# Ways in and out of a long convolution as fixed rounds, with the ranking of its mixture of experts moved into the middles

## Chip, cores and metric

The kernel runs on one core of a Trainium2 chip. The metric is the device time of one execution in microseconds, the median of three runs.

## What is computed

A gated long convolution in fp32 feeds a two-level mixture of experts. Shapes: 4 batches, 10048 positions, 128 channels; the experts' stage sees 40192 tokens, 4 groups of 4 experts, hidden size 1024.

```python
h_filt = (relu(pos_emb @ w1) @ w2) * exp(-0.01 * pos)[:, None]
u = x * v
y = irfft(rfft(u, 2 * S) * rfft(h_filt, 2 * S))[:, :S]
t = (x * y).reshape(B * S, D)
g = argmax(t @ w_group); e = argmax(t @ w_expert[g])
out = g_weight * e_weight * (relu(t @ w1[g, e]) @ w2[g, e])
```

## The kernel before

The transform is done by matmuls, and one batch of 128 channels fits into two tiles in SBUF, `z` and `zr` (frequencies from 64 on). Each batch passes through three kinds of work, all in `conv`:

- the way in: 43 parts of 3 channels. `product` loads x and v (tile `xv`, SP's queue, line 462) and multiplies them on VectorE (line 467); ScalarE writes a negated half (line 478) and VectorE folds both into `eo` (line 480), which is `fold`. `dft_blocks` multiplies `eo` with a table on TensorE (line 412, 6 matmuls a part, two instructions each), and ScalarE copies the result into `z` and `zr` (line 425).
- the middle, or way through: 40 steps over pairs of frequencies. `middle` transforms over positions (line 497), multiplies with the filter's spectrum on VectorE (lines 660 and 663, tile `t`), and POOL adds (lines 661 and 664, tile `y`); `back` transforms back (line 673), and ScalarE copies into `z` (line 680).
- the way out: 22 groups of 6 channels (the last two of 4), two groups sharing one set of transposes. `turned` transposes `z` on TensorE (lines 692 and 695) and copies to tiles `tt` on ScalarE (line 697), `inverse_rest` starts the sums for two `po` buffers (line 707), `inverse_blocks` loads `xo`, the other factor, from `x_out` (line 723, ScalarE's queue; line 725, SP's, for the last batch), finishes the sums (line 728), has ScalarE copy halves crosswise into `oo` (lines 737 and 738), adds on VectorE (`yt`, line 743) and multiplies with `xo` into `xy` (line 745).

The way in of batch b and the way out of batch b - 1 are one loop over the 22 groups. In this text, way 1 is batch 1 in and batch 0 out, middle 1 the way through of batch 1, and so on to way 3 and middle 3; the last way only goes out.

Beside this runs the routing of the batch before. `chosen` sends `xy` to DRAM, computes the router's logits and picks experts; `ranked` (line 857) gives every token its row in a table of pages: about 80 to 110 VectorE instructions, most of them on 128x16 tiles, some two dozen on 128x316 ones. Both are generators; `next(routing, None)` in `conv` takes a step. A step of `chosen` is taken 22 times, so in a middle of 40 places, 27 of which take a step, 5 steps of `ranked` come in the middle, the rest in the next way, one in each group.

When `ranked` has the addresses, it appends to `self.scatters`: 8 clears (line 393) and 79 puts (line 378), indirect DMAs that POOL issues, 128 rows of 520 bytes each. `scatter` sends some at each step, each after ScalarE's latest copy (`pace`); `stage` loads the rows (`stg`, line 367).

The order on each engine comes from a scheduler (the tile layer) that may move an instruction ahead of another. `keep_in_program_order` (called through `in_turn`, too) holds the instructions so marked in the order written. Before, VectorE's product and fold, ScalarE's copies of line 425 and the first matmul of a way are marked; transposes, inverse matmuls, `oo`, `yt` and `xy` are not.

Of the kernel before, what the change touches and what calls it, by code (L numbers as in the profile page):

```python
# [149 lines left out]
class Kernel:  # L150
# [60 lines left out]
    def conv(self, ctx, right):  # L211
# [27 lines left out]
        for b in range(self.nbat + 1):  # L239
            last = b == self.nbat  # L240
            if last:
                ahead.close()
                inner.close()
                self.sp = ctx.enter_context(tc.tile_pool(name="stream", bufs=2, reuse_waits="tile"))
                weights = self.first_weights(right)
            if b > 0:
                xy = xyp.tile([128, NB, D], F32, tag="xy", name=f"xy{b - 1}")
            parts = groups(D, GD) if not last else []
            if b == 1:
                self.router_consts()  # L250
            self.run_ahead(b, 0, made, folded)
            for j, (d0, n) in enumerate(OUTS):
                if b > 0 and j % 2 == 0:
                    tts = self.turned(d0, min(2 * GI, D - d0))
                for i in range(2 * j, min(2 * j + 2, len(parts))):
                    self.run_ahead(b, i, made, folded)
                    self.scatter(1 + (i >= 12 and i % 2))
                    self.dft_blocks(*folded[i])
                    if b > 0 and i % 2 == 0:
                        if j % 2 == 0:  # L260
                            pos = self.inverse_rest(min(2 * GI, D - d0), tts)
                        self.inverse_blocks(b - 1, xy, d0, n, tts, pos[j % 2], j % 2)
                if last:
                    if j % 2 == 0:
                        pos = self.inverse_rest(min(2 * GI, D - d0), tts)
                    self.inverse_blocks(b - 1, xy, d0, n, tts, pos[j % 2], j % 2)
                    next(weights, None)
                    if j == 8:
                        self.scatter(sum(1 for s in self.scatters if s[0] < self.nbat - 2))
                        for p in self.all[:XG]:  # L270
                            p.load()
                for _ in range(3 if last else 1):
                    next(routing, None)
                if last:
                    self.scatter(1 + j % 2)
            made, folded = [], []
# [127 lines left out]
    def dft_blocks(self, b, eo, d0, n, other=False):  # L404
# [4 lines left out]
        for i in range(n):  # L409

            for h, hs in enumerate(HALVES):
# [3 lines left out]
                if d0 == i == h == 0 and b not in ("h", 0):  # L415
                    self.tc.keep_in_program_order(ins)
# [14 lines left out]
    def run_ahead(self, b, i, made, folded):  # L431
# [4 lines left out]
        while len(folded) < min(len(parts), i + AHEAD + 1):  # L436
            folded.append(self.fold(*made[len(folded)]))
# [6 lines left out]
    def product(self, b, d0, n):  # L444
# [15 lines left out]
        else:  # L460
# [3 lines left out]
            if b > 0:  # L464
                self.minus[d0] = xv[:, :n].rearrange("p d a q -> p d (a q)")
        first = b == 0 and d0 < FIRST
        self.in_turn(b, (nc.gpsimd if first else nc.vector).tensor_tensor(xt, xt, vt, ALU.mult))
        return xt, b, d0, n

    def fold(self, xt, b, d0, n):  # L470
# [5 lines left out]
        if b:  # L476
            both = self.minus.pop(d0)
            self.in_turn(b, nc.scalar.activation(both[:, :, 128:192], hi, AF.Copy, scale=-1.0))
# [203 lines left out]
    def turned(self, d0, n):  # L682
# [4 lines left out]
        for s, m in [(None, n // 4)] + groups(n, 4):  # L687
            pt = self.psT.tile([128, 4, 128], F32, tag="pt", name="pt")
            for i in range(m):
                if s is None:  # L690
                    src = self.zr[:, d0 + 4 * i : d0 + 4 * i + 4].rearrange("p d k s -> p (d k s)")
                    nc.tensor.transpose(pt[:, i], src, self.ident)
                else:
                    src = self.z[:, d0 + s + i].rearrange("p k s -> p (k s)")
                    nc.tensor.transpose(pt[:, i], src, self.ident)
# [3 lines left out]
        return tts  # L699

    def inverse_rest(self, n, tts):

        pos = [self.psO.tile([128, GI, NB], F32, tag="po", name="po") for _ in range(2)]
        for g in range(n // 4):
            for h, hs in enumerate(HALVES):
                for po, rs in zip(pos, HALVES):
                    self.nc.tensor.matmul(
# [5 lines left out]
                    )  # L713
        return pos

    def inverse_blocks(self, b, xy, d0, n, tts, po, run):

        nc, d, sp = self.nc, self.d, self.sp
        rows = lambda t: t[:, : n * NB].rearrange("p (t d) -> p t d", d=n)
        xo = sp.tile([128, GI * NB], F32, tag="spec", name="xo", bufs=NSPEC - (b == self.nbat - 1))  # L720
        src = d["x_out"][b, :, d0 * NB : (d0 + n) * NB]
        if b < self.nbat - 1:
            nc.scalar.dma_start(xo[:, : n * NB], src)
        else:
            self.tc.keep_in_program_order(nc.sync.dma_start(xo[:, : n * NB], src))
        for c in range(n):
            for h, hs in enumerate(HALVES):
                nc.tensor.matmul(
                    po[hs, c],
                    tts[1 + c // 2][:, 2 * run + c % 2, hs],  # L730
                    self.fi[:, h, 0],
                    start=False,
                    stop=c == n - 1,
                )
        oo = rows(sp.tile([128, GI * NB], F32, tag="oo", name="oo"))
        by_row = po[:, :n].rearrange("p d t -> p t d")
        nc.scalar.activation(oo[0:64], by_row[64:128], AF.Copy, scale=-1.0)
        ins = nc.scalar.copy(oo[64:128], by_row[0:64])
        if b == self.nbat - 1:
            self.pace = ins  # L740
        pool, tag, bufs = (self.ap, "y", NY) if b < self.nbat - 1 else (sp, "yt", 2)
        yt = rows(pool.tile([128, GI * NB], F32, tag=tag, name="yt", bufs=bufs))
        nc.vector.tensor_tensor(yt, by_row, oo, ALU.add)
        helped = b == self.nbat - 1 and d0 // GI % 2 > 0
        ins = (nc.gpsimd if helped else nc.vector).tensor_tensor(
            xy[:, :, d0 : d0 + n], yt, rows(xo), ALU.mult
        )
        if helped:
            self.beyond(ins)


# [105 lines left out]
    def ranked(self, b, oh, en):  # L857
# [4 lines left out]
        v = nc.vector  # L862
# [320 lines left out]

class Unit:
# [274 lines left out]
```

## Time and profile before

| what | value |
|---|---|
| median of three runs | 2073.45 us (2071.23 to 2076.63) |
| the profiled execution, its own time | 2074.26 us |
| its span | 2072.5 us |
| TensorE matmuls / weight loads busy | 1933.1 us (93%) / 1756.5 us (85%) |
| VectorE / ScalarE / POOL busy | 1592.8 / 1424.9 / 1304.2 us |
| DMA | 391.34 MB, 189 GB/s on average |
| first expert matmul starts (line 1307) | 1003.8 us |

The span runs from the profile's first to its last instruction; the execution's own time is 1.8 us longer. The filter and batch 0's way in and middle fill the first 249 us, the ways and middles of this text the stretch from there to 976 us, and the experts' stage is the rest, from about 1004 us on. Busy shares over the whole span are averages over stages with different limits, so a stage has to be read by itself. A busy TensorE is not one at its peak, since matmuls overlap and their ends are modelled.

### The profile page before, as it was taken

The numbers are of one execution on the slowest core, as the hardware profiler recorded it, in microseconds if no ns is written. First come the engines' busy times: TensorE is split into PE (matmuls) and PEld (weight loads), VectorE is DVE, ScalarE is ACT, GpSimd is POOL, SyncE is SP. The second block draws the span as 40 slices with busy tenths as digits, with TensorE's granted clock in tenths as the row PEclk, the third lists the DMA queues.
The fourth block names the chain that finished last, engine by engine and source line by source line (L and its number), as shares of the span: only waits on it lengthen the run. The fifth ranks groups of instructions, "written<-read, shape, count | busy, mean of one in ns | idle before, by whom it ended". The sixth has DMA issues, their size and how long they took to land. (4 is left out here: it accounts for less than half of the span.)

```text
span 2072.5 us, 53304 instructions
## 1 busy us (share of the span) xinstructions
PE 1933.1 (93%) x17518; PEld 1756.5 (85%) x17518; DVE 1592.8 (77%) x3478; ACT 1424.9 (69%) x3395; POOL 1304.2 (63%) x1355
## 2 busy tenths in 40 slices
PE   8988999988898889987999999999999999999997
PEld 7877888777676767766798999999999999999997
DVE  5587676796569855882799997777999998888885
ACT  6652487456543654345787888878888888888885
POOL 3257602655698457956276777878888886555554
PEclk9999999999999999988899999999999999999998
DMA  4699877977897778856654455555555544444442
GB/s 136 224 268 268 260 193 243 309 210 213 228 331 225 219 207 289 288 172 199 219 184 136 142 147 149 155 180 154 162 156 160 156 144 128 134 123 127 127 121 65
DMA packets 260158, 391.34 MB, mean 189 GB/s; under 512 B 32839, under 2 KB 132914, under 8 KB 259872
## 3 DMA queue, kind: packets, MB, share of 16 engines
q1 hardware_dynamic: 226464, 320.47, 51.9%
q0 software_dynamic: 23904, 51.83, 7.2%
q10 hardware_dynamic: 9504, 15.54, 2.8%
q8 instruction: 142, 2.33, 0.5%
q14 instruction: 144, 1.18, 0.2%
HBM read 305.70 MB, written 83.04 MB: 188 GB/s over the span
## 5 line engine op out<-in xcount | busy, mean ns | idle before, releaser
L1316 DVE SCALAR_TENSOR_TENSOR hl<-ph,hh 128x512 fp32r<-128x512 f32 x656 | 446.0, 685 | 126.5 <-ACT hh L1315 98.3
L1315 ACT ACTIVATE hh<-ph 128x512 fp32r<-128x512 f32 x656 | 395.0, 606 | 137.4 <-PE ph L1309 54.2
L378 POOL DMA_INDIRECT prow<-stg,adr x316 | 342.7, 1084 | 153.8 <-issue 60.3
L1352 POOL DMA_INDIRECT out<-os,to x328 | 355.2, 1083 | 92.5 <-issue 81.3
L1326 PE MATMUL py<-hh,wh 128*128 128x256 f32 x1312 | 398.0, 303 | 0.0
L1307 PE MATMUL ph<-xh,wh 128*128 128x256 f32 x1312 | 373.2, 284 | 7.9 <-DVE hl L1316 4.5
L1328 PE MATMUL py<-hh,wl 128*128 128x256 f32 x1312 | 372.4, 284 | 7.3 <-POOL wl L1296 7.3
L1309 PE MATMUL ph<-xh,wl 128*128 128x256 f32 x1312 | 373.4, 285 | 0.3 <-DVE wl L1296 0.3
L1308 PE MATMUL ph<-xl,wh 128*128 128x256 f32 x1312 | 372.6, 284 | 0.0
L1327 PE MATMUL py<-hl,wh 128*128 128x256 f32 x1312 | 370.8, 283 | 0.0
L1296 POOL TENSOR_TENSOR wl<-ws,wh 128x512 fp32r<-128x512 f32 x162 | 218.9, 1351 | 214.5 <-ACT wh L1289 166.5
L1307 PEld LDWEIGHTS ph<-xh,wh 128*128 128x128 f32 x1312 | 252.4, 192 | 8.9 <-ACT hh L1315 4.6
L1328 PEld LDWEIGHTS py<-hh,wl 128*128 128x128 f32 x1312 | 250.7, 191 | 10.0 <-POOL wl L1296 9.9
L1309 PEld LDWEIGHTS ph<-xh,wl 128*128 128x128 f32 x1312 | 252.7, 193 | 1.2 <-DVE wl L1296 1.2
L1308 PEld LDWEIGHTS ph<-xl,wh 128*128 128x128 f32 x1312 | 252.7, 193 | 0.1
L1327 PEld LDWEIGHTS py<-hl,wh 128*128 128x128 f32 x1312 | 252.1, 192 | 0.0
L1326 PEld LDWEIGHTS py<-hh,wh 128*128 128x128 f32 x1312 | 251.3, 192 | 0.0
L1296 DVE TENSOR_TENSOR wl<-mw,wh 128x512 fp32r<-128x512 f32 x318 | 231.1, 727 | 0.0
L1289 ACT CAST wh<-ws 128x512 fp32r<-128x512 f32 x328 | 206.8, 630 | 9.1 <-PE ph L1309 7.1
L412 PE MATMUL psa<-fa,eo 96*64 96x158 f32 x2048 | 194.0, 315 | 18.6 <-issue 6.1
L661 POOL TENSOR_TENSOR y<-t 128x256 f32<-128x256 f32 (+1 forms) x160 | 120.3, 752 | 143.6 <-DVE t L660 138.9
L1289 ACT CAST wh<-mw 128x512 fp32r x318 | 202.4, 637 | 0.0
(231 smaller groups left out, 4073.6 us busy)
## 6 DMA issues: line engine op xcount, KB each, us to landing
ws<-m_w SPq DMA_DIRECT2D x328, 256.0 KB
ht<-hspec SPq DMA_DIRECT2D x156, 256.0 KB
xv<-xv_in SPq DMA_DIRECT2D x131, 288.0 KB
bt<-c_b SPq DMA_DIRECT2D x95, 256.0 KB
xg<-prow SPq DMA_DIRECT2D x164, 130.0 KB
bp<-c_bp SPq DMA_DIRECT2D x76, 256.0 KB
xyd<-xy SPq DMA_DIRECT2D x76, 256.0 KB
stg<-xyd SPq DMA_DIRECT2D x76, 256.0 KB
```

Source lines behind the costliest of these rows:

```text
L378: ins = self.nc.gpsimd.indirect_dma_start(self.d["prow"], bass.IndirectOffsetOnAxis(ap=u.adr[:, t : t + 1], axis=0), u.rows[:, t - u.t0], ...
L1289: k.fix(k.nc.scalar.copy(hi, self.matrix(i, half, self.ea)))
L1296: ins = v.tensor_tensor(lo, self.matrix(i, half, self.ed), self.wh[i][half].bitcast(F32), ALU.subtract)
L1307: k.fix(nc.tensor.matmul(ph[:, j], wh, self.xh, start=True, stop=False))
L1308: k.fix(nc.tensor.matmul(ph[:, j], wh, self.xl, start=False, stop=False))
L1309: k.fix(nc.tensor.matmul(ph[:, j], wl, self.xh, start=False, stop=True))
L1315: k.fix(nc.scalar.activation(hh, ph, AF.Relu))
L1316: k.fix(nc.vector.scalar_tensor_tensor(hl, ph, 0.0, hh.bitcast(F32), ALU.max, ALU.subtract))
L1326: k.fix(nc.tensor.matmul(self.py, wh, self.hh[c], start=(c == 0), stop=False))
L1327: k.fix(nc.tensor.matmul(self.py, wh, self.hl[c], start=False, stop=False))
L1328: k.fix(nc.tensor.matmul(self.py, wl, self.hh[c], start=False, stop=(c == NC - 1)))
L1352: ins = k.nc.gpsimd.indirect_dma_start(k.d["out"], bass.IndirectOffsetOnAxis(ap=self.to[:, h : h + 1], axis=0), o[:, h], None, bounds_chec ...
```

## The change

Four things are done.

- The loop of a way becomes rounds of two groups. In a round, TensorE gets transposes (all but the last four), the forward matmuls of two parts, the last four transposes, the remainder, one group's inverse matmuls, two parts more, and the other group's inverse matmuls. All of these, and the copies, `oo`, `yt` and `xy` behind them, are marked to keep program order. `yt` and `xy` of a group are put off (`finish`) to a place in the next group. The fourth `tt` copy of a round goes to VectorE; in the last way the first does, too, and three transposed blocks use the buffers of `psA`.
- `xo` is loaded by `gate`, always on SP's queue, one group ahead. For batches after the first, the negated half is written right behind the product, and one part fewer is folded ahead.
- A middle takes a step of `routing` at each of its 40 places. `ranked` marks its VectorE instructions by a wrapper, `InTurn` (they then all show as line 1221). The steps that followed a middle are gone.
- Scatters in a middle go one at each of the first 24 places, where they were three of four places over all 40.

```diff
+            finish, xos = [], []
             for j, (d0, n) in enumerate(OUTS):
+                both = min(2 * GI, D - d0)
                 if b > 0 and j % 2 == 0:
-                    tts = self.turned(d0, min(2 * GI, D - d0))
+                    tts = self.turned(d0, both, last, False)
+                if b > 0:
+                    for o in OUTS[max(j + (j > 0), 0) : j + 2]:
+                        xos.append(self.gate(b - 1, *o))
                 for i in range(2 * j, min(2 * j + 2, len(parts))):
                     self.run_ahead(b, i, made, folded)
                     self.scatter(1 + (i >= 12 and i % 2))
+                    if i % 2 == j % 2:
+                        self.finish(finish)
                     self.dft_blocks(*folded[i])
-                    if b > 0 and i % 2 == 0:
-                        if j % 2 == 0:
-                            pos = self.inverse_rest(min(2 * GI, D - d0), tts)
-                        self.inverse_blocks(b - 1, xy, d0, n, tts, pos[j % 2], j % 2)
+                if b > 0:
+                    self.finish(finish)
+                    if j % 2 == 0:
+                        if not last:
+                            tts += self.turned(d0, both, last, True)
+                        pos = self.inverse_rest(both, tts)
+                    finish.append(self.inverse_blocks(b - 1, xy, d0, n, tts, pos[j % 2], j % 2, xos.pop(0)))
                 if last:
-                    if j % 2 == 0:
-                        pos = self.inverse_rest(min(2 * GI, D - d0), tts)
-                    self.inverse_blocks(b - 1, xy, d0, n, tts, pos[j % 2], j % 2)
                     next(weights, None)
...
-                    self.scatter(i % 4 != 3, False)
-                    if i % 4 != 3 if i < 30 else i in (31, 33):
-                        next(routing, None)
+                    self.scatter(i < 24, False)
+                    next(routing, None)
...
-                for _ in range(2):
-                    next(routing, None)
...
-        while len(folded) < min(len(parts), i + AHEAD + 1):
+        while len(folded) < min(len(parts), i + AHEAD + (b == 0)):
...
-    def turned(self, d0, n):
+    def turned(self, d0, n, last, late):
...
-        for s, m in [(None, n // 4)] + groups(n, 4):
-            pt = self.psT.tile([128, 4, 128], F32, tag="pt", name="pt")
+        parts = [(None, n // 4)] + groups(n, 4)
+        if not last and n == 2 * GI:
+            parts = parts[-1:] if late else parts[:-1]
+        elif late:
+            return []
+        for s, m in parts:
+            own = last and s is not None and s > 0
+            pool, tag = (self.psA, "ps") if own else (self.psT, "pt")
+            pt = pool.tile([128, 4, 128], F32, tag=tag, name="pt")
...
-            nc.scalar.copy(tt[:, :m], pt[:, :m])
+            other = late or last and (s is None or s + m == n)
+            copy = nc.vector.tensor_copy if other else nc.scalar.copy
+            self.tc.keep_in_program_order(copy(tt[:, :m], pt[:, :m]))
...
+    def gate(self, b, d0, n):
+
+        xo = self.sp.tile([128, GI * NB], F32, tag="spec", name="xo", bufs=NSPEC - (b == self.nbat - 1))
+        src = self.d["x_out"][b, :, d0 * NB : (d0 + n) * NB]
+        self.tc.keep_in_program_order(self.nc.sync.dma_start(xo[:, : n * NB], src))
+        return xo
+
+    def finish(self, steps):
+
+        while steps:
+            steps.pop(0)()
...
-        v = nc.vector
+        v = nc.vector if fine else InTurn(nc.vector, tc)
```

What this does to the orders is seen at three places. TensorE in way 2, from the middle of the way: `psa` is the forward matmul's result, `pt` a transpose's, `po` the sum of the way out (158 columns for the remainder, 79 for the inverse). Before:

```order
L412 MATMUL psa<-fa,eo 64x158 x6
L707 MATMUL po<-fi,tt 64x158 x12
L728 MATMUL po<-fi,tt 64x79 x24
L692 MATMUL pt<-ident,zr 128x128 x3
L695 MATMUL pt<-ident,z 128x128 x12
L707 MATMUL po<-fi,tt 64x158 x6
L728 MATMUL po<-fi,tt 64x79
L412 MATMUL psa<-fa,eo 64x158 x12
L728 MATMUL po<-fi,tt 64x79 x6
L412 MATMUL psa<-fa,eo 64x158 x12
```

and now:

```order
L706 MATMUL pt<-ident,zr 128x128 x3
L706 MATMUL pt<-ident,z 128x128 x8
L417 MATMUL psa<-fa,eo 64x158 x12
L706 MATMUL pt<-ident,z 128x128 x4
L736 MATMUL po<-fi,tt 64x158 x12
L753 MATMUL po<-fi,tt 64x79 x12
L417 MATMUL psa<-fa,eo 64x158 x12
L753 MATMUL po<-fi,tt 64x79 x12
```

The second piece is one whole round, and it repeats through ways 1 to 3; before, the scheduler had split and joined these groups differently from round to round.

VectorE near the end of middle 2: `t` are the products with the filter's spectrum, the 128x16, 128x2 and 128x316 rows are the ranking. Before:

```order
L663 TENSOR_TENSOR t_8708<-psb,ht 128x512
L888 TENSOR_SCALAR need<-need 128x16
L660 TENSOR_TENSOR t_8725<-psb,ht 128x512
L892 TENSOR_SCALAR ni<-need 128x16
L663 TENSOR_TENSOR t_8728<-psb,ht 128x512
L893 TENSOR_SCALAR ni<-ni 128x16
L467 TENSOR_TENSOR xv<-xv 96x3x128
L894 TENSOR_SCALAR ni<-ni 128x16
L660 TENSOR_TENSOR t_8747<-psb,ht 128x512
```

and now:

```order
L665 TENSOR_TENSOR t_8823<-psb,ht 128x512
L1221 TENSOR_TENSOR oh<-oh,c_8538 128x4
L1221 TENSOR_TENSOR lt<-f,thr 128x316
L1221 TENSOR_SCALAR et<-et 128x2
L668 TENSOR_TENSOR t_8826<-psb,ht 128x512
L1221 TENSOR_TENSOR lt<-lt,dlt 128x316
L1221 TENSOR_TENSOR et<-et,ec 128x2
L1221 TENSOR_SCALAR ev<-iota,fend 128x2
L1221 TENSOR_TENSOR f<-f,lt 128x316
L1221 TENSOR_TENSOR et<-et,ev 128x2
L665 TENSOR_TENSOR t_8843<-psb,ht 128x512
```

The wide rows, which stood in way 3, now stand between the last products of the middle.

VectorE in the last way, `yt` and `xy` of two groups. Before:

```order
L743 TENSOR_TENSOR yt<-po,oo 128x474
L745 TENSOR_TENSOR xy_11976<-yt,xo 128x79x6
L743 TENSOR_TENSOR yt<-po,oo 128x474 x2
L745 TENSOR_TENSOR xy_11976<-yt,xo 128x79x6
L743 TENSOR_TENSOR yt<-po,oo 128x474 x2
```

and now:

```order
L774 TENSOR_TENSOR xy_12055<-yt,xo 128x79x6
L710 COPY tt<-pt 128x384
L710 COPY tt<-pt 128x512
L772 TENSOR_TENSOR yt<-po,oo 128x474 x2
L774 TENSOR_TENSOR xy_12055<-yt,xo 128x79x6
```

Two copies of transposed blocks have come in ahead of each pair of `yt`.

In the ways POOL sends 46 puts in way 2 and 43 in way 3 before, 50 in each now; in middles 2 and 3 30 each before, 24 now.

## Rows read from the trace of the kernel before

**Rows 1.** Windows, experts' stage: length, busy PE, PEld, DVE, ACT, POOL, clock, DMA share, GB/s.

```profile
1900.00:1950.00 50.00, 50.00 (x422) 50.00 (x421) 40.30 (x88) 43.00 (x97) 28.18 (x26) 1.00 0.42 126
```

**Rows 2.** Windows by stage: way 1, middle 1, way 2, and so on.

```profile
249.00:343.00 94.00, 90.12 (x1421) 77.92 (x1422) 62.88 (x119) 76.92 (x208) 1.42 (x3) 0.98 0.67 182
343.00:441.00 98.00, 92.65 (x601) 73.00 (x597) 78.20 (x177) 42.12 (x101) 64.98 (x87) 0.99 0.91 293
441.00:561.00 120.00, 102.49 (x1440) 83.92 (x1440) 77.59 (x174) 78.39 (x211) 64.71 (x66) 0.96 0.76 212
561.00:668.00 107.00, 98.25 (x585) 75.38 (x586) 85.44 (x192) 42.43 (x101) 95.31 (x119) 0.95 0.91 288
668.00:787.00 119.00, 103.84 (x1424) 85.31 (x1422) 79.40 (x188) 76.23 (x203) 60.14 (x60) 0.93 0.72 201
787.00:890.00 103.00, 94.50 (x586) 73.01 (x585) 78.83 (x161) 41.16 (x97) 91.76 (x117) 0.97 0.85 280
890.00:976.00 86.00, 70.83 (x958) 58.17 (x958) 46.28 (x127) 47.53 (x92) 48.80 (x52) 0.86 0.58 181
```

**Rows 3.** Windows: pieces of middles 1 and 2 and of ways 2, 3, last.

```profile
400.00:441.00 41.00, 35.92 (x183) 28.58 (x181) 40.54 (x109) 15.15 (x34) 28.24 (x35) 0.99 0.82 247
...
490.00:561.00 71.00, 57.41 (x763) 45.43 (x761) 35.37 (x68) 43.13 (x118) 40.68 (x45) 0.94 0.77 208
561.00:620.00 59.00, 58.60 (x400) 45.84 (x401) 38.40 (x69) 26.26 (x65) 52.18 (x67) 0.96 0.93 316
620.00:668.00 48.00, 39.65 (x187) 29.55 (x186) 47.05 (x124) 16.17 (x36) 43.13 (x53) 0.93 0.88 254
...
710.00:787.00 77.00, 64.72 (x881) 51.77 (x877) 41.44 (x83) 47.25 (x131) 43.10 (x47) 0.93 0.76 206
890.00:930.00 40.00, 33.72 (x370) 27.10 (x371) 33.09 (x105) 18.77 (x36) 17.05 (x19) 0.79 0.62 196
```

**Rows 4.** Windows of line 412 alone: TensorE's busy us and count, second pieces.

```profile
490.00:561.00 71.00, 28.11 (x272) 20.52 (x272) 0.94 0.77 208
...
710.00:787.00 77.00, 33.59 (x332) 24.50 (x332) 0.93 0.76 206
```

**Rows 5.** Waits in way 1: engine, line, releaser; total us, times, longest.

```profile
PEld po L728 <- issue: 0.9, 4, 0.2
```

**Rows 6.** Waits in way 2.

```profile
PEld po L728 <- issue: 10.0, 22, 1.3
```

**Rows 7.** Timeline of TensorE in way 3: start, us, what, count, idle before.

```profile
750.33 0.37 PE L728 MATMUL po<-fi,tt 128*64 128x79 f32 x4 [0.43 <-issue]
```

**Rows 8.** Groups of ScalarE in way 2: busy us, mean ns, idle us before.

```profile
L697 ACT COPY tt<-pt 128x512 f32<-128x512 f32 (+2 forms) x43 | 21.7, 569 | 5.1 <-PE pt L695 3.0 <-PE psa L412 1.2 <-PE pt L692 0.7
```

**Rows 9.** Timeline of SP's queue, a stretch of way 1.

```profile
290.82 25.90 SPq L462 DMA_DIRECT2D xv<-xv_in  x13
```

**Rows 10.** Timeline of SP's queue, a stretch of way 3.

```profile
734.01 4.49 SPq L462 DMA_DIRECT2D xv<-xv_in  x3
...
744.74 3.43 SPq L462 DMA_DIRECT2D xv<-xv_in  x3
```

**Rows 11.** Timeline of TensorE, transposes of line 692 in the last way.

```profile
949.37 0.55 PE L692 MATMUL pt<-ident,zr 128*128 128x128 f32 x3
...
966.22 0.44 PE L692 MATMUL pt<-ident,zr 128*128 128x128 f32 x2
```

**Rows 12.** Timeline of VectorE, one round of the last way.

```profile
961.74 0.65 DVE L745 TENSOR_TENSOR xy<-yt,xo 128x474 f32<-128x474 f32 x1
962.31 0.65 DVE L743 TENSOR_TENSOR yt<-po,oo 128x474 f32<-128x474 f32 x1
```

**Rows 13.** Waits in the last way.

```profile
PEld pt L695 <- ACT tt L697: 11.0, 7, 2.8
```

**Rows 14.** Timeline of VectorE, end of middle 2.

```profile
659.79 0.16 DVE L914 TENSOR_SCALAR base<-start 128x16 f32<-128x16 f32 x1
...
660.34 1.79 DVE L915 TENSOR_TENSOR base<-base,rem 128x16 f32<-128x16 f32 x1
```

More of the change, by code (lines that the diff above doesn't have):

```diff
@@ L275, in conv @@
                     self.scatter(1 + j % 2)
+            self.finish(finish)
             made, folded = [], []
@@ L414, in dft_blocks @@
                 )
-                if d0 == i == h == 0 and b not in ("h", 0):
+                if b not in ("h", 0):
                     self.tc.keep_in_program_order(ins)
@@ L463, in product @@
             xt, vt = xv[:, :n, 0], xv[:, :n, 1]
-            if b > 0:
-                self.minus[d0] = xv[:, :n].rearrange("p d a q -> p d (a q)")
         first = b == 0 and d0 < FIRST
         self.in_turn(b, (nc.gpsimd if first else nc.vector).tensor_tensor(xt, xt, vt, ALU.mult))
+        if b > 0:
+            both = self.minus[d0] = xv[:, :n].rearrange("p d a q -> p d (a q)")
+            self.in_turn(b, nc.scalar.activation(both[:, :, 128:192], xt[:, :, 64:128], AF.Copy, scale=-1.0))
         return xt, b, d0, n
@@ L713, in inverse_rest, with inverse_blocks @@
                     )
+                    self.tc.keep_in_program_order(ins)
         return pos
[L716 to L725, printed above, removed]
+    def inverse_blocks(self, b, xy, d0, n, tts, po, run, xo):
+        nc, sp, turn = self.nc, self.sp, self.tc.keep_in_program_order
+        last = b == self.nbat - 1
@@ L726, in inverse_blocks @@
         for c in range(n):
             for h, hs in enumerate(HALVES):
[L728 to L733, printed above, removed]
+                turn(
+                    nc.tensor.matmul(
+                        po[hs, c],
+                        tts[1 + c // 2][:, 2 * run + c % 2, hs],
+                        self.fi[:, h, 0],
+                        start=False,
+                        stop=c == n - 1,
+                    )
@@ L734, in inverse_blocks @@
                 )
-        oo = rows(sp.tile([128, GI * NB], F32, tag="oo", name="oo"))
+        oo = self.per_row(sp.tile([128, GI * NB], F32, tag="oo", name="oo"), n)
         by_row = po[:, :n].rearrange("p d t -> p t d")
-        nc.scalar.activation(oo[0:64], by_row[64:128], AF.Copy, scale=-1.0)
+        turn(nc.scalar.activation(oo[0:64], by_row[64:128], AF.Copy, scale=-1.0))
         ins = nc.scalar.copy(oo[64:128], by_row[0:64])
-        if b == self.nbat - 1:
+        turn(ins)
+        if last:
@@ L740, in inverse_blocks, with finish @@
             self.pace = ins
[L741 to L749, printed above, removed]
+        def finish():
+            pool, tag, bufs = (sp, "yt", 2) if last else (self.ap, "y", NY)
+            yt = self.per_row(pool.tile([128, GI * NB], F32, tag=tag, name="yt", bufs=bufs), n)
+            turn(nc.vector.tensor_tensor(yt, by_row, oo, ALU.add))
+            helped = last and d0 // GI % 2 > 0
+            ins = (nc.gpsimd if helped else nc.vector).tensor_tensor(
+                xy[:, :, d0 : d0 + n], yt, self.per_row(xo, n), ALU.mult
+            )
+            self.beyond(ins) if helped else turn(ins)
@@ L752, in first_of_max @@
+        return finish
     def first_of_max(self, lg, n, name):
@@ L1181, in fetch, with __init__, __getattr__, call @@
             self.spare -= 1
+class InTurn:
+    def __init__(self, engine, tc):
+        self.engine, self.tc = engine, tc
+    def __getattr__(self, name):
+        def call(*args):
+            ins = getattr(self.engine, name)(*args)
+            self.tc.keep_in_program_order(ins)
+            return ins
+        return call
 class Unit:
```

8 lines of the change are left out of this document (4 added, 4 removed).

## The prediction, made before the changed kernel ran

> **What bounds the kernel now.** The experts' stage is TensorE's: a 50 us stretch of it has 50.00 us of matmuls and 50.00 of weight loads [rows 1]. The change leaves it alone, so I read what stands before it: first busy time by stage [rows 2], then by pieces of a stage [rows 3], then one line's progress, waits and single instructions in the slow pieces.
>
> Way 1 (batch 1 in, batch 0 out) takes 94 us with TensorE busy 90.12. Ways 2 and 3 do the same transforms and take 120 and 119 us [rows 2]. Two things are in them that way 1 lacks: the ranking on VectorE (77.59 and 79.40 us busy against 62.88, so 14.7 and 16.5 us) and the scatter on POOL (64.71 and 60.14 us against 1.42). Their second pieces show which costs more. VectorE has room there, 35.37 of 71 us and 41.44 of 77 [rows 3], and still the forward matmuls of line 412 get on by only 272 of 512 in 71 us and 332 in 77 [rows 4]: whole ways at that pace would take 134 and 119 us. TensorE's sequencer stops there for "issue": before the inverse matmuls of line 728 it does so for 0.9 us in way 1 [rows 5] and 10.0 in way 2 [rows 6]; in one such stop four matmuls run and then 0.43 us pass [rows 7]. The profile names no engine that they wait for. They come with puts in flight, and hardly without.
>
> A middle ("way through") has two halves. In the first, POOL and DMA are near their limits once there are puts (52.18 of 59 us, share 0.93). In the second it is VectorE: 40.54 of 41 us in middle 1, 47.05 of 48 in middle 2 [rows 3]. What VectorE gets more to do there is paid in full.
>
> **The change, part by part.** The sum is made against the profiled execution, 2074.26 us (span 2072.5 and 1.8 around it); the median of the runs, 2073.45, is 0.8 lower. About 0.3% (6 us) is what a measurement here can tell from no change.
>
> *Ranking moved.* In the built order the ranking rows among a middle's products grow from 21 to 79, 22 to 82 and 14 to 72; 4 are left for way 2, but 29 and 41 still stand in way 3 and in the last way. They need the last choice, so they come where VectorE is full. Middle 1 pays what way 2 had, 14.7 us; one fold fewer run ahead gives 0.5 back: **+14**. Middles 2 and 3 each take some 60 rows of way 3's 91, 60 / 91 x 16.5 = 11 us. They lose the puts of their second half, too (30 in a middle become 24, all in its first 24 steps): the second half of middle 2, with 12 of them, took 48 us for what middle 1 did in 41, so some 6 come back, while 6 more in the first half bring POOL from 52.18 of 59 us to its limit, some 3. **+8** each, bounds 0 and +20.
>
> *Ways as rounds.* TensorE gets transposes, forward twelves, remainder and inverse in one fixed cycle. Way 1 was already busy 90.12 of 94: **-2**, bounds -4 and +3. ScalarE gives one of four tt copies to VectorE: 11 of 0.57 us [rows 8], 6 us in a way where VectorE has 31 to spare. xo's issue goes from ScalarE's queue to SP's, one group ahead: 0, covered by that group; were it late, xy would be, which frees a spec buffer only groups later. The delayed yt and xy cost 0: a po buffer is wanted back at the next remainder, after 15 transposes and a forward twelve; if ScalarE fell behind by more than that, TensorE would wait there.
>
> Ways 2 and 3 are the open cost. From below: way 1's pace, 92, the puts costing nothing. From above: the pace of the second pieces, 119 and more. A value between comes from DMA: way 2's queues are busy for 0.76 x 120 = 91 us, way 1's for 0.67 x 94 = 63, so 0.5 us for each of 54 scatters more; with 4 puts more way 2 needs 93, and way 3 0.72 x 119 + 7 x 0.5 = 89. At the share of middles 1 and 2, 0.91 [rows 2], that is 102 and 98; way 3 has ranking left at its start, +3. I take **101 for both: -19 and -18**, nearest to what the queues allow, since the rounds should even out loads: way 1 issues 13 without a break [rows 9], way 3 three at a time [rows 10].
>
> *Last way.* 86 us. Its first 40 us hold ranking (VectorE 33.09 busy [rows 3]); three rounds later on take 16.85 us, 5.6 each [rows 11]. The new order has two tt copies on VectorE ahead of a round's late yt, where yt followed xy at once [rows 12]: 2 x 0.57 later, less the 0.25 that TensorE waited after it anyway, so 6.5 a round, +10 in 11 rounds. Against that, 58 of 99 ranking rows leave the start, 58 x 16.5 / 91 = 10.5 us of VectorE, of which I count 7, as it was not quite full; and the transposes, now in more buffers, no longer wait for tt copies, 11.0 us [rows 13], of which I count 7, since the other rounds had hidden part. **-4**, bounds -17 and +8.
>
> The experts' stage starts with as many puts to do (139 become 140): 0.
>
> Sum: +14 +8 +8 -2 -19 -18 -4 = -13, so 2074.3 - 13 = **2061 us**.
>
> **A rule against it.** In middle 2 the 128x16 subtraction of line 915 took 1.79 us, and the row of the same shape two before it 0.16 [rows 14]. The Trainium skill, SBUF — State Buffer, section Who interferes with whom, says that a VectorE instruction with two inputs in SBUF and a GpSimd instruction that reads SBUF shut each other out for a whole instruction. By that rule most of the ranking would queue behind POOL's additions once it stands in a middle. The trace agrees for this row; what it would cost in full is rival (c).
>
> **Rivals.** (a) *The rounds free the puts of their cost*: the stops came from bursts of loads, and ways 2 and 3 run at 93, so 8 less each: **2045**. For it: way 1 has the same loads and no stop. Against: DMA would have to be busy nearly all the time. The Trainium skill, DMA: Bandwidth & Descriptors, section Queues, rings and completion order, has each DMA engine take turns between the queues that have work; xo leaving ScalarE's queue leaves one competitor fewer, which speaks for (a). No row here shows it.
>
> (b) *Slower: the stops stay.* Puts now run from the first round to the last, at the rate that only the second pieces had. If they hold TensorE as there, ways 2 and 3 stay near 120, and the middles pay all the same: 2061 + 2 x 19 = **2099**. It decides above 101 + 13 / 2, so when ways 2 and 3 take over 107 us. For it: as many puts in a round as now. Against: the bursts of [rows 10].
>
> (c) *Slower: the ranking queues behind POOL.* If each row that moves is held on average 0.2 us, an eighth of what line 915 lost, that is 12 us a middle for 58 rows: 2061 + 3 x 12 = **2097**. It decides at 0.07 us a row. Against: without puts POOL is busy 28.24 of 41 us there, not 43.13 of 48 [rows 3].
>
> (d) *The change doesn't do what it says*: partly so, a third of the rows stays in way 3 and the last way; that is in the sum.
>
> **How the numbers follow.** Forecast 0.40, (a) 0.25, (b) 0.21, (c) 0.14. The forecast's own range, by its bounds, is 2045 to 2080. To hold 8 in 10 the range takes in (a) with 9 more from way 1 and the last way, 2036, and of (b) and (c) what falls short of their full price: **2036 to 2094**. Faster: 0.27 of the forecast, 0.23 of (a), 0.02 of (b): 0.52. No change: 0.10, 0.02, 0.04 and 0.03: 0.19. Slower: 0.03, 0.15 and 0.11: 0.29.
>
> **What would show it.** Right: middles of 112, 115 and 111 us, VectorE over 95% busy in their second halves; ways 2 and 3 at 98 to 104, with "issue" before the inverse matmuls halved; the last way at 80 to 84, its rounds 6.5. Wrong: middles under 108 (then VectorE did not bound them), ways 2 and 3 over 107 (b), 128x16 rows of the ranking at 0.3 us and more in the middles (c), or a change in the experts' stage, for which I have no term.

## Result and profile after

| | before | after |
|---|---|---|
| median of four runs each, us | 2075.04 (2071.23 to 2079.75) | 2096.29 (2092.79 to 2107.81) |
| ratio, 95% interval | | 1.0113 (1.0074 to 1.0151) |
| profiled execution: time / span, us | 2074.26 / 2072.5 | 2107.81 / 2105.6 |

The change makes the kernel 1.1% slower. The forecast was 2061 us; the result lies just above the range and close to rivals (b), 2099, and (c), 2097. The profiled execution of after is the longest of its four, 11.5 us above their median, so the stages below add up to more than the median's loss.

Busy time by stage of after: way 1, middle 1, and so on, then what lies between the last way and the experts, and the experts' stage (columns as in [rows 2]).

```profile
250.10:336.30 86.20, 86.18 (x1440) 76.75 (x1440) 68.61 (x129) 71.31 (x199) 0.80 (x2) 1.00 0.75 207
336.30:448.20 111.90, 99.11 (x580) 74.16 (x578) 95.04 (x229) 41.88 (x99) 64.86 (x87) 0.93 0.76 249
448.20:577.00 128.80, 110.94 (x1441) 91.95 (x1441) 70.25 (x133) 73.68 (x201) 63.92 (x72) 0.90 0.72 207
577.00:690.50 113.50, 97.85 (x582) 73.22 (x581) 95.91 (x232) 41.54 (x97) 87.34 (x110) 0.94 0.79 257
690.50:814.80 124.30, 108.64 (x1440) 88.81 (x1440) 77.21 (x155) 72.98 (x201) 67.70 (x69) 0.90 0.73 211
814.80:927.50 112.70, 97.48 (x582) 72.61 (x582) 93.61 (x220) 40.48 (x95) 89.31 (x113) 0.95 0.75 247
927.50:1001.00 73.50, 56.95 (x928) 48.37 (x928) 41.52 (x87) 33.99 (x62) 43.55 (x46) 0.96 0.65 199
1001.00:1030.80 29.80, 23.18 (x259) 14.61 (x259) 15.07 (x65) 19.32 (x56) 6.33 (x9) 0.94 0.54 194
1030.80:2105.60 1074.80, 1031.58 (x8534) 1019.66 (x8534) 866.23 (x1908) 874.29 (x1971) 736.08 (x672) 0.99 0.48 146
```

A stage is measured here from its first transposes to its last inverse matmul (a middle is what lies between); the kernel before is cut at the same places, so some bounds lie a few us from those of [rows 2].

| stage | before | after | difference | forecast |
|---|---|---|---|---|
| way 1 | 94.4 | 86.2 | -8.2 | -2 |
| middles 1, 2, 3 | 97.4, 105.6, 104.2 | 111.9, 113.5, 112.7 | +14.5, +7.9, +8.5 | +14, +8, +8 |
| ways 2, 3 | 119.4, 123.3 | 128.8, 124.3 | **+9.4, +1.0** | **-19, -18** |
| last way, choice behind it | 77.2, 32.8 | 73.5, 29.8 | -3.7, -3.0 | -4 |
| experts' stage | 1068.7 | 1074.8 | +6.1 | 0 |

Way 1 is now TensorE's alone, 86.18 of 86.20 us, in rounds of 8.1 us. In the middles' second halves VectorE is busy for 99% of the time; middles 1 and 2:

```profile
396.00:448.20 52.20, 39.67 (x145) 28.25 (x143) 51.91 (x144) 13.46 (x27) 29.96 (x39) 0.84 0.57 172
...
637.00:690.50 53.50, 37.85 (x148) 26.92 (x146) 53.23 (x150) 13.39 (x27) 34.26 (x42) 0.88 0.60 183
```

Ways 2 and 3 have the same matmuls as way 1 at a granted clock of 0.90 instead of 1.00. Their first three rounds take 10.5, 9.0, 8.1 and 10.0, 10.8, 9.0 us. From the fourth on, where the loop sends six scatters in a round on average and not four, they take 8 to 15.5, mostly by turns near 10.5 and near 15: rounds of 14 us and more hold seven to nine puts and clears, those near 10.5 four to six. TensorE's weight loads wait for "issue" (us in total, times, longest; before: [rows 5, 6]), first in way 1:

```profile
PEld po L753 <- issue: 0.4, 2, 0.2
```

The same waits in way 2:

```profile
PEld po L753 <- issue: 15.5, 32, 1.2
PEld psa L417 <- issue: 9.1, 24, 1.2
```

A stop of way 2 in the timeline (start, us, instruction, count, idle before), first POOL:

```profile
491.52 1.06 POOL L383 DMA_INDIRECT prow<-stg,adr  x1 [3.01 <-issue]
492.88 0.98 POOL L383 DMA_INDIRECT prow<-stg,adr  x1 [0.30 <-issue]
494.17 1.20 POOL L383 DMA_INDIRECT prow<-stg,adr  x1 [0.30 <-ACT tt L710]
495.67 0.97 POOL L383 DMA_INDIRECT prow<-stg,adr  x1 [0.30 <-issue]
496.63 0.35 POOL L375 COPY stg<-en 128x8 f32<-128x8 f32 x1
497.15 1.12 POOL L383 DMA_INDIRECT prow<-stg,adr  x1 [0.16 <-issue]
498.58 0.97 POOL L383 DMA_INDIRECT prow<-stg,adr  x1 [0.30 <-issue]
```

TensorE in the same stretch:

```profile
494.79 0.58 PE L753 MATMUL po<-fi,tt 128*64 128x79 f32 x6
495.75 0.27 PE L753 MATMUL po<-fi,tt 128*64 128x79 f32 x1 [0.39 <-issue]
496.48 0.36 PE L753 MATMUL po<-fi,tt 128*64 128x79 f32 x4 [0.46 <-issue]
497.21 0.37 PE L753 MATMUL po<-fi,tt 128*64 128x79 f32 x3 [0.37 <-issue]
497.92 0.40 PE L753 MATMUL po<-fi,tt 128*64 128x79 f32 x4 [0.34 <-issue]
```

POOL sends six puts with 0.3 us or less of idle time between them. From 495.4 us on, after the third, TensorE gets at most four matmuls and then pauses, once in some 0.72 us; the six just before took 0.58. Every pause for issue of over 0.25 us in ways 2 and 3 of this trace has two or more puts or clears begun in some 4 us ahead of it, most have three; way 1 has no such pause. Grouped by what POOL sends with at most 0.7 us between, the seven groups of six have 3 to 7 of these pauses each, the 14 groups of three 0 to 2. Open is whether it is the puts' number, their order in time, or the loads beside them.

A stop also costs TensorE afterwards. Windows of this one and of the 5 us behind it:

```profile
495.00:500.00 5.00, 2.51 (x25) 1.48 (x22) 2.56 (x5) 0.67 (x3) 3.77 (x5) 0.98 1.04 285
500.00:505.00 5.00, 4.87 (x47) 4.76 (x46) 2.24 (x4) 2.96 (x8) 1.78 (x2) 0.50 0.76 198
```

TensorE is busy for 2.51 of 5 us, and then works at a granted clock of 0.50, the lower of its two levels (1.2 GHz). Of the 42.6 us that way 2 takes over way 1, 17.8 are idle time and 24.8 a longer busy time for the same matmuls; at a granted clock of 0.90 the clock's part is an estimated 0.10 x 128.8 = 13 us. Against the kernel before, cut at the table's places, way 2's idle time is much the same (17.9 us for 16.9); what it gained is busy time, 110.9 us for 102.4, at a granted clock of 0.90 for 0.96.

### The profile page after: what moved, and what is told of

Its sections match the earlier page's. It is cut to its first block, busy times and chain, and to the rows that moved or that the text cites. A ratio compares the mean times of both kernels' runs of the same rounds, so it can differ in the third digit from the quotient of the medians.

```text
span 2105.6 us, 53322 instructions
## 1 busy us (share of the span) xinstructions
PE 1939.1 (92%) x17518; PEld 1755.2 (83%) x17518; DVE 1595.6 (76%) x3530; ACT 1395.8 (66%) x3343; POOL 1286.1 (61%) x1355
## 4 chain that ended last, share of the span: by engine, by line
PE 45%; ACT 2%; issue 2%; DVE 1%; DMA 1%; ACTq 0%; POOL 0%; SPq 0%; DVEq 0%; POOLq 0%
PE ph L1353 7%; PE py L1372 7%; PE ph L1351 7%; PE ph L1352 7%; PE py L1370 7%; PE py L1371 7%; PE ptm L1384 2%; PE px L1306 1%; ACT hh L1359 1%; ACT ys L1377 1%; ACT wh L1333 0%; PE ptr L839 0%; PE plt L847 0%; ACTq L1275 0%; DVE hl L1360 0%
## 5 line engine op out<-in xcount | busy, mean ns | idle before, releaser
L383 POOL DMA_INDIRECT prow<-stg,adr x316 | 332.7, 1053 | 162.5 <-issue 65.3
L1333 ACT CAST wh<-ws 128x512 fp32r<-128x512 f32 x328 | 208.1, 634 | 16.7 <-PE ph L1353 13.1
L417 PE MATMUL psa<-fa,eo 96*64 96x158 f32 x2048 | 184.2, 320 | 16.1 <-issue 7.3
```

The lines of the kernel that those rows point to most:

```text
L383: ins = self.nc.gpsimd.indirect_dma_start(self.d["prow"], bass.IndirectOffsetOnAxis(ap=u.adr[:, t : t + 1], axis=0), u.rows[:, t - u.t0], ...
L1333: k.fix(k.nc.scalar.copy(hi, self.matrix(i, half, self.ea)))
```

## Experiments

Times of one chip are compared with the kernel before on that chip, since chips differ (next part). "Sends" are puts and clears together.

**One scatter at each part.** In the changed kernel:

```diff
-                    self.scatter(1 + (i >= 12 and i % 2))
+                    self.scatter(1)
...
-                    self.scatter(i < 24, False)
+                    self.scatter(i < 39, False)
```

> The changed kernel, but with one scatter at each part of a way all through (from the 13th part on every second part had two), and 39 places of a middle with a put, not 24. Scatters in ways 2 and 3 fall from 58 to 43 each; the middles take the other 15. Theory B (bursts): TensorE stops when POOL issues four or more puts back to back, which rounds with 6 scatters make it do. In the changed kernel the rounds of ways 2 and 3 with 4 scatters took 10.5, 9.0, 8.1 and 10.0, 10.8, 9.0 us (mean 9.6), those with 6 about 12.6. At 9.6 in 10.7 rounds ways 2 and 3 come to about 102 us each, from 129 and 124. The middles pay 0 to 5 us each. Total 2096 - 49 + 0 to 10 = 2047 to 2057. Theory P (each scatter costs TensorE the same, (126.5 - 86.2) / 58 = 0.7 us): 10 us less in each way, 2076 to 2086. Theory L (the loads of xv and xo do it, the puts only happen beside it): ways as they are, about 2096.

The kernel before took 1998.48 us on this chip, some 75 less than where it was first measured. On it: 2031.88 us, 1.0166 (1.0147 to 1.0186) of before there, ways 2 and 3 at 90.6 and 92.4, middles 2 and 3 at 123.7 and 119.3. None of its ways has a pause for issue of over 0.2 us, so this run can't decide between the theories.

**No scatters in way 3.** The same place with `self.scatter(1 if b < 3 else 0)`, a put at all 40 places of a middle, and `self.scatter(4)` in the last way.

> The changed kernel, but way 3 sends nothing, way 2 one scatter at each part, middle 2 a put at each of 40 places, middle 3 almost none (the clears of batch 1 stand first in its list), and the last way, with four at each group, gets what is left (137). Only stages up to middle 3 are to be read. Theories B and P: way 3 takes what way 1 takes, 86 to 89 us, with no stops for issue over 0.25 us. Theory L: way 3 stays at 115 to 125. Way 2 with 43 scatters: B 102, P 118, L 129. Middle 3 without puts: 108 to 113 if VectorE alone bounds its second half, 103 or less if the puts slow VectorE there.

On the same chip, way 3 and middle 3:

```profile
664.70:755.20 90.50, 88.44 (x1440) 78.36 (x1440) 76.34 (x155) 71.89 (x200) 0.00 (x0) 0.98 0.70 197
755.20:860.10 104.90, 96.36 (x583) 72.89 (x581) 88.06 (x220) 40.84 (x95) 64.22 (x85) 0.95 0.73 238
```

Way 3 takes 90.5 us with ranking still at its start; with 43 sends it took 92.4 on that chip (e1). Way 2, the same in both kernels, took 94.0 and 90.6, so on this chip the spread sends have no price that can be told. Middle 3, with 4 puts, takes 104.9, and VectorE is busy 88.06 us for the same work that takes it 99.82 in e1 with 39 puts, on the same chip; with some 24 puts, in two executions of the changed kernel on other chips, it is 93.61 and 89.34.

**The two kernels on other chips.** No edit; to see what the chip does in it.

> The changed kernel itself, on another chip than the one its first profile came from, where the kernel before takes 1998 us and not 2074, to tell the chip's part in ways 2 and 3 from the kernel's. With one scatter a part these ways took 90.6 and 92.4 us there, with ranking back in the ways and 46 to 49 puts 101.9 and 106.0. If the stops (theory B) are as long on every chip: ways 2 and 3 at 120 to 129, middles at 112 to 114, about 2070. If the stops are much shorter on this chip: ways 2 and 3 at 95 to 105, middles the same, about 2025, and the ratio to the kernel before is about what it was, 1.01 to 1.02, since the middles pay on both.

> The kernel before itself, for a profile on the same chip as the other runs. Its time there is 1998 us, 75 less than where its first profile was taken. If the stops are what differs: ways 2 and 3 at 95 to 105 (119.4 and 123.3 there), middles and the experts' stage within 3 us of 97, 106, 104 and 1069. If the difference is spread over all stages, as a slower clock or slower memory would do, every stage is 3 to 4% shorter.

> The changed kernel. On a chip with stops as it was twice: 2096 to 2110, ways 2 and 3 at 124 to 129. On a chip without them: ways 2 and 3 at 93 to 100, middles as before at 112 to 114, experts' stage 1056, total 2030 to 2040, and the kernel before 1998: then the change loses its middles and wins little back in the ways.

> The kernel before, for its profile on the same chip. With stops: as twice, 2074. Without: 1998, where ways 2 and 3 should be what differs, 95 to 105 us each in place of 120 and 123, and the experts' stage at 1055 to 1060 in place of 1069.

> The changed kernel. On a chip with stops as three times before: 1.011 to 1.016 of the kernel before. On a chip without them: ways 2 and 3 at 92 to 102, middles 112 to 116, experts 1055, total 2030 to 2040, so 1.015 to 1.02: the middles pay there too and the ways of the kernel before had less to lose.

> The kernel before, for its profile. On a chip without stops (1998 us): ways 2 and 3 at 92 to 105 in place of 120 and 123, middles unchanged at 97, 106, 104, experts 1055. On a chip with stops: 2074 as before.

| chip | before, us | after, us | ratio (95%) | ways 2, 3 before | ways 2, 3 after |
|---|---|---|---|---|---|
| e6, e7 | 2074.34 | 2109.20 | 1.0160 (1.0113 to 1.0207) | 120.6, 123.3 | 127.3, 126.3 |
| e10, e11 | 2074.10 | 2105.76 | 1.0144 (1.0109 to 1.0179) | 121.7, 122.8 | 124.2, 122.1 |
| e17, e18 | 2091.10 | 2107.70 | 1.0084 (1.0043 to 1.0124) | 122.9, 122.7 | 130.1, 121.9 |

None of the three was like the chip of e1. The result holds on all three, with the same middles (112 to 113, 113 to 116, 108 to 114) and way 1 at 86.2. The experts' stage is 1066.6 to 1086.1 in four profiles of before and 1073.6 to 1077.2 in four of after, so its +6.1 cannot be told from the scatter. The chip of e1, e2, e3 and e5, and one more below (e14, e15), show no pause for issue of over 0.2 us ahead of TensorE's matmuls in any way ("without stops" from here on); the kernel before takes 1998 us there. Neither kernel of the case has a profile on one, and what the change is worth there stays open.

**One scatter at each part, beside the changed kernel.** The kernel of e1 on a chip with stops (that of e10).

> The same kernel as e1_one_put, beside the changed kernel on one chip. So far TensorE's stops were seen on two chips (the kernel before takes 2074 us there, 8 to 10 us of stops for issue of over 0.25 us in way 2) and not on the third (1998 us, none). On a chip with stops: theory B (bursts) ways 2 and 3 at 88 to 102 us and 25 to 45 us less than the changed kernel in total, the middles paying 7 to 10 us more each; theory P (every put costs TensorE there) 116 and 114 us, total the same within 5 us of the changed kernel. On a chip without stops: as before, 90.6 and 92.4.

2070.55 us, 0.9986 (0.9964 to 1.0009) of before, 35 us less than the changed kernel. Way 2, middle 2, way 3 and middle 3 there, by windows, of the changed kernel:

```profile
450.30:574.50 124.20, 108.44 (x1441) 88.59 (x1441) 70.12 (x132) 73.44 (x201) 64.83 (x72) 0.91 0.74 214
574.50:690.20 115.70, 101.08 (x581) 75.51 (x581) 97.96 (x233) 41.62 (x98) 87.08 (x110) 0.90 0.78 253
690.20:812.40 122.20, 108.36 (x1440) 87.82 (x1440) 77.03 (x154) 71.85 (x197) 65.13 (x69) 0.91 0.75 214
812.40:920.40 108.00, 95.13 (x582) 71.97 (x582) 89.34 (x220) 41.70 (x97) 87.35 (x113) 0.98 0.77 258
```

The same four of the one-put kernel:

```profile
444.10:547.60 103.50, 96.33 (x1440) 81.44 (x1440) 69.31 (x131) 71.19 (x198) 47.59 (x53) 0.97 0.81 236
547.60:671.40 123.80, 102.48 (x581) 73.53 (x581) 103.49 (x233) 42.51 (x101) 105.62 (x129) 0.92 0.79 253
671.40:772.20 100.80, 94.33 (x1440) 80.20 (x1440) 76.67 (x154) 72.19 (x199) 53.67 (x51) 0.98 0.81 235
772.20:892.00 119.80, 100.50 (x581) 72.71 (x581) 98.97 (x220) 41.07 (x95) 105.42 (x131) 0.95 0.76 253
```

15 sends fewer in each way save 21 us, more than the 10 that a fixed price a send would give ((123.2 - 86.2) / 58 = 0.64 us each), and pauses for issue fall from 11.5 to 2.4 us in way 2. Of way 2's 20.7 us, 12.1 are busy time, at a granted clock of 0.97 instead of 0.91. The 15 puts more cost middles 2 and 3 8 and 12 us.

**Sends in bursts.** The one-put kernel with `self.scatter(8 * (i % 8 == 5))`: 40 sends in a way, eight at a time.

> The one-put kernel (ways 2 and 3 at 103.5 and 100.7 us on a chip with stops), with its scatters in a way bunched: eight at every eighth part, none between, so 40 in place of 43 in a way, but in bursts. To be read on a chip with stops only (on the chip without them: ways at 90 to 93). Theory B (bursts): eight in a row hold POOL 10 us, of which TensorE is stopped or slowed in the last 6; five bursts cost 3 to 5 us each, so ways 2 and 3 at 112 to 120, rounds by turns near 8.5 and 13. Theory N (the number of puts in a round decides, however they follow): 40 sends, so 98 to 104 us.

> The bunched kernel beside the one whose puts write nothing, on one chip. On a chip with stops: ways 2 and 3 at 125 to 140 us again.

Ways 2 and 3 by windows, on a chip with stops:

```profile
448.00:585.00 137.00, 119.83 (x1440) 95.63 (x1440) 69.47 (x132) 73.53 (x200) 43.75 (x49) 0.80 0.63 178
705.90:834.00 128.10, 110.87 (x1440) 89.33 (x1440) 76.64 (x155) 73.11 (x200) 44.80 (x48) 0.86 0.67 191
```

Three sends fewer than in the spread kernel, and 137 and 128 us instead of the 103.5 and 100.8 of e8 on another chip. On this chip way 3 with spread sends, in e13 below, took 95.5. So the order in time decides, not the number. Rounds that send take 10.8 to 16.7 us, but for one of 8.1. In way 2 the granted clock of 0.80 alone is an estimated 0.20 x 137 = 27 us. On a chip without stops (e15) the same kernel took 97.9 and 100.9, still 7 and 8 us more than the spread one in e1 on another such chip; what that part comes from was not found.

**Bursts whose rows don't travel.** In that kernel, so that nearly all rows of batches 0 and 1 are left out of the table:

```diff
-            bounds_check=n - 1,
+            bounds_check=n - 1 if u.b > 1 else 0,
...
-        q0 = self.nbat * SEQ // TP
+        q0 = 0
```

> The bunched kernel, but the puts of batches 0 and 1, those sent in ways 2 and 3, have a bound of 0, so that nearly all their rows fall outside and are not written (middle 1 clears the whole table instead, and gets longer). POOL issues as many puts in the same bursts; the rows no longer travel. Left out: the rows of batches 0 and 1 in the result. Theory W (the write traffic of a burst is what stops TensorE): ways 2 and 3 at 88 to 96 us, apart from the eight clears in each, which still write. Theory Q (POOL's issuing is): ways as in the bunched kernel, 128 to 137. On the chip without stops nothing can be read.

> The bunched kernel whose puts of batches 0 and 1 write nothing, once more, since the chip it ran on had no stops (bunched 97.9 and 100.9 us in ways 2 and 3 there, without the writes 95.5 and 98.5). On a chip with stops, where bunched puts gave 136.9 and 128.1: theory W (the rows that travel stop TensorE) 90 to 98 us; theory Q (POOL's issuing does) 125 to 137.

The first run fell on a chip without stops (95.5 and 98.5 us). The second did not; its ways 2 and 3 by windows:

```profile
519.20:661.20 142.00, 117.97 (x1440) 94.59 (x1440) 68.01 (x127) 73.38 (x199) 43.37 (x49) 0.79 0.57 154
782.50:918.80 136.30, 112.99 (x1440) 90.28 (x1440) 76.78 (x155) 73.01 (x200) 44.17 (x48) 0.83 0.60 165
```

A stop in its timeline of TensorE:

```profile
646.81 0.36 PE L753 MATMUL po<-fi,tt 128*64 128x79 f32 x4 [0.49 <-issue]
648.28 0.40 PE L753 MATMUL po<-fi,tt 128*64 128x79 f32 x2 [1.11 <-issue]
649.72 0.41 PE L753 MATMUL po<-fi,tt 128*64 128x79 f32 x2 [1.03 <-issue]
```

The software queue in its way 2 (packets, MB, share of 16 engines):

```profile
q0 software_dynamic: 1664, 2.15, 4.3%
```

The same queue in way 2 of the kernel whose rows travel:

```profile
q0 software_dynamic: 1664, 4.26, 8.9%
```

As many packets, half the bytes (the clears still write), and the stops are no shorter, though on another chip: 142 and 136 us, with 24.0 us of pauses for issue in way 2 where e12 had 16.1. So it is not the written rows. What is left is POOL's issuing of indirect DMAs, or the handling of their descriptors; no run tells these two apart.

**The kernel before with one scatter at each part.** The first edit, in the kernel before, with `self.scatter(1, False)` in a middle.

> The kernel before, with the same edit of the puts alone: one scatter at each part of a way, a put at every place of a middle. Theory B holds for its ways as well: 120 and 123 us become 102 to 108 on a chip with stops, since 4 sends stand in a round there too. Middles 2 and 3 pay for 9 puts more each, at 0.6 us, 5 us. Total 2074 - 32 + 10 = 2045 to 2060. If the stops in the kernel before come from its bursts of loads and not from puts: ways as they are, and 2080 to 2085.

2066.23 us, 0.9964 (0.9940 to 0.9988). Its ways 2 and 3:

```profile
437.70:538.10 100.40, 92.04 (x1440) 79.00 (x1440) 77.03 (x173) 76.31 (x207) 44.75 (x47) 0.98 0.78 226
...
654.10:762.50 108.40, 98.89 (x1444) 83.33 (x1444) 80.79 (x194) 77.29 (x207) 57.14 (x51) 0.96 0.76 212
```

From the 120 to 123 of other chips down to 100 and 108, with its loads still in bursts (twelve without a break in way 3): the ways of before, too, lost their time to bursts of puts. The ways' sends fall by 15 and 8 as well, but in e12 their number was not what counts.

**Ranking taken back.** In the changed kernel, steps of `ranked` as before and without `InTurn`; alone (e3, e9), and with the one-put edit (e5).

```diff
-                    next(routing, None)
+                    if i % 4 != 3 if i < 30 else i in (31, 33):
+                        next(routing, None)
...
+                for _ in range(2):
+                    next(routing, None)
```

> The changed kernel, but the steps of ranking are taken as in the kernel before (27 of 40 places in a middle, two after it, the rest in the ways) and its VectorE instructions are not held in order; rounds and scatters stay. The middles should fall from 111.8, 113.5, 112.7 to about 97, 103, 102, so 36 us less. In the ways VectorE gets 16 us more: if what holds ways 2 and 3 is TensorE's stops, this is hidden (VectorE 70 and 77 of 129 and 124 us) and they stay within 4 us; the last way pays 5 to 10. Total 2096 - 36 + 8 = 2065 to 2075. If VectorE's work in a way is paid in full: 2096 and more.

> The same kernel as e3_rank_back, beside the changed kernel on one chip. On a chip with stops: middles at 96, 105, 100, as they do not depend on stops; ways 2 and 3 at 120 to 130 if the stops hide the ranking, 135 and more if not; the last way at 98. Total 2075 to 2090. On a chip without stops: 2030 again.

> Both edits of the two other kernels: rounds kept, ranking steps as in the kernel before, one scatter at each part of a way and 39 puts in a middle. If theory B holds and ranking is hidden in a way, ways 2 and 3 take 100 to 107 us (VectorE then 86 of them busy), the middles 97 to 108, total 2096 - 36 - 45 + 8 + 0 to 12 = 2023 to 2035. If theory P: 2055 to 2065. If theory L: 2065 to 2080.

On a chip with stops 2093.75 us, 1.0093 (1.0063 to 1.0124); without, 1.0163 (1.0132 to 1.0195), and with one put 1.0238 (1.0221 to 1.0255). Middle 1, way 2 and the last way of e9:

```profile
335.90:432.10 96.20, 92.58 (x580) 73.29 (x578) 77.62 (x176) 41.73 (x99) 64.89 (x87) 0.98 0.88 287
432.10:563.80 131.70, 111.00 (x1441) 92.75 (x1441) 84.67 (x185) 73.24 (x200) 61.49 (x67) 0.88 0.70 199
...
897.60:996.80 99.20, 65.16 (x932) 53.66 (x932) 53.91 (x128) 33.92 (x62) 46.07 (x49) 0.86 0.48 150
```

Middles fall to 96.2, 103.6 and 102.1 us, so ranking alone is their 16, 12 and 6 us (against e10). But ways 2 and 3 pay 7.5 and 6, and the last way 25: its ranking stands on VectorE ahead of the ordered tt, yt and xy, and the first two rounds take 13 and 21 us. With one put at each part (e5 against e1, on one chip) the middles give back 16.1, 8.7 and 6.0 us, and ways 2, 3 and the last way pay 11.4, 10.0 and 22.9. There only the first batch is worth taking back, and that was tried:

> The one-put kernel (2070.6 us, 0.9986 of the kernel before), with the ranking of the first batch alone taken back into way 2. Middle 1 falls from 112 to 96; way 2 pays 8 to 12, as it did where all ranking was taken back. So 4 to 8 us less: 0.994 to 0.997 of the kernel before on a chip with stops.

2063.81 us, **0.9947 (0.9920 to 0.9975)** of before on a chip with stops. Its ways 2 and 3 (middle 1 is back at 96.1 us):

```profile
431.10:535.80 104.70, 94.27 (x1440) 80.81 (x1440) 83.55 (x184) 71.32 (x198) 45.13 (x47) 0.97 0.77 224
...
661.20:756.70 95.50, 91.35 (x1440) 79.18 (x1440) 76.50 (x154) 71.72 (x199) 52.20 (x51) 0.99 0.84 248
```

It beats the kernel before there; the changed kernel has no run on this chip. No gain can be told over the kernel before with one scatter at each part (e4: 2066.23 us on this chip, runs of 2053.9 to 2071.1; here 2057.2 to 2070.8), so what is gained may be the spacing alone. On a chip without stops it was not run.

## Why the prediction was wrong

- **Ways 2 and 3: the step that failed.** "I take 101 for both", because DMA's queues allow 102 and 98, and "the rounds should even out loads". Measured +9.4 and +1.0 for -19 and -18: this is rival (b), decided as it said, above 107 us. Its "for" (as many puts in a round) named the puts, rightly, but by their number; what counts is how closely they follow each other. 40 sends in bursts give 128 us in way 3 where 43 spread give 95.5 on the same chip. Its "against" (bursts of loads, [rows 10]) was not the cause: the kernel before still has such bursts and falls to 100 and 108 once its puts are spread. The rows to price it by were there: [rows 4, 6] had been read as "they come with puts in flight", and then the sum was made by how much DMA carries. At the forecast's DMA share of 0.91 the ways would have taken 101 us; the slowest ways here have shares of 0.57 to 0.67. Nor had the sum a term for TensorE's clock, which stood at 0.90 in both ways.
- **Middles: right, in cause and size.** +14.5, +7.9, +8.5 for +14, +8, +8, with VectorE busy for 99% of the second halves. With the ranking taken back (e9) the middles fall by 16, 12 and 6 us.
- **Rival (c)** is not needed for that sum, and its sign, 128x16 rows at 0.3 us and more, did not come. These rows took 0.28, 0.24 and 0.23 us on average in middles 1, 2 and 3, against 0.17 to 0.18 in ways 2 and 3 of before; at 35 to 41 rows a middle that is 2 to 4 us, a part of (c)'s 12. That POOL and VectorE hold each other up is seen at the puts, too: in middle 3 the ranking rows take VectorE 27.2 us with the changed kernel's 24 puts, which are sent ahead of most of the ranking, 27.2 with 4 (e2), and 32.5 with 39 (e1, on the chip of e2). The Trainium skill, SBUF — State Buffer, section Who interferes with whom, which the forecast cited, agrees in kind.
- **Way 1: -8.2 for -2, beyond the bound of -4.** The forecast took 90.12 busy of 94 as a floor. The same matmuls (90.94 us for all 1440) are now busy 86.18: a busy TensorE was not one at its peak.
- **Last way: -3.7 for -4**, and 3.0 more behind it. Its rounds, foreseen at 6.5 us against 5.6 [rows 11], take 6.3, as two of them show below. That the sum fits is in part luck: terms of +10 for the rounds and -14 for ranking and transposes stand against -5.4 measured in the first five rounds (35.5 us for 40.9) and +1.6 in the other six (37.9 for 36.3).

```profile
957.10 1.47 PE L706 MATMUL pt<-ident,z 128*128 128x128 f32 x12
...
963.41 1.47 PE L706 MATMUL pt<-ident,z 128*128 128x128 f32 x12
```

- **Experts' stage: 0 foreseen**, +6.1 in this execution; by the profiles of other chips not to be told from none.

With ways 2 and 3 at what they took, the forecast's other terms give 2061 + 37 + 10 = 2108, and way 1 gives 6 back: 2102, where this execution took 2107.8 and the median 2096.3.

## What to carry to other kernels

When an engine pauses for "issue" only while another engine does one thing, price the pauses by how that thing is bunched, before reasoning from bandwidth: send as many in other spacing, and see. Count what follows a pause, too: here the granted clock fell behind it. Work that is moved off a stalled stage into one whose bound it loads is paid there in full, and frees only part of it in the stalled stage: the first two batches' ranking cost the middles 16 and 12 us and freed 7.5 and 6 in ways 2 and 3 (e9 against e10). Compare kernels on one chip only, and see whether a second chip shows the stall at all.

## What the hardware showed

- Indirect DMAs that POOL issues back to back (1.0 to 1.4 us each, 0.3 between) hold TensorE, in the two stops shown from about the third on and until the burst ends: to one to four matmuls per 0.72 us in the changed kernel, to two per 1.45 us at times in e16, where nearly no rows were written. Five sets of runs on chips showed it, two on others did not.
- Behind a stop that left TensorE busy for 2.51 of 5 us, the granted clock was 0.50 (1.2 GHz) for the next 5 us. Way 2 had a granted clock of 0.97 with spread puts, 0.91 with the changed kernel's and 0.80 with bursts of eight.
- A refill of instructions in flight is not what it waits for. In 493 to 501 us of after, with the stop above, the queues moved (packets, MB, share of 16 engines):

```profile
q1 hardware_dynamic: 1207, 1.80, 85.3%
q0 software_dynamic: 157, 0.33, 13.7%
q14 instruction: 1, 0.01, 0.3%
```

  No packet of q8, the queue of 16 KB instruction packets, is in it; the next comes at 502.6 us, when the stop is over. The one packet of q14, 8 KB, took 0.4 us. The Trainium skill, Runtime: NRT & Kernel Launch, section Instruction fetch mechanics, has engines refill in 16 KiB blocks by a DMA queue of their own; by that rule TensorE had its block. What the stop does wait for was not found.
- The kernel before takes 1998 us on some chips and 2074 to 2091 on others; only the latter had the stops. That these make the whole difference is not shown: the experts' stage differs, too, with 1055.4 to 1059.2 us in e1, e3, e5 and e15, without stops, and 1066.6 to 1086.1 in the eight profiles of both kernels, with them.
